# Polysketch attention and a SwiGLU block on one core: chunk 1's weight splits on VectorE ahead of the numerators' copy, and two moves around the first later unit

## The chip, the cores and the metric

The kernel runs on one core of a Trainium2 chip. The metric is the device time of one execution in microseconds, the median of several runs. The times of the profile come from one profiled execution of the same program.

## The reference

Four batches of four heads, 1088 positions and head size 32 go through an attention with sketched features; the result (4352 tokens of 128 values) goes through a gated feed-forward block with 1536 hidden columns.

```python
def phi(x):
    a = einsum('rd,bhsd->bhsr', S1, x); b = einsum('rd,bhsd->bhsr', S2, x)   # r = 8
    return einsum('bhsi,bhsj->bhsij', a, b).reshape(..., 64)
kv  = einsum('bhsf,bhsd->bhfd', phi(k), v);  z = phi(k).sum(axis=2)
num = einsum('bhsf,bhfd->bhsd', phi(q), kv)
den = einsum('bhsf,bhf->bhs', phi(q), z)[..., None] + 1e-06
x   = (num / den).transpose(0, 2, 1, 3).reshape(4352, 128)
g   = x @ w_gate
out = (g / (1 + exp(-g)) * (x @ w_val)) @ w_out
```

## The kernel before

The feed-forward block works on the transposed tokens `xT`, 128 values by 4352 tokens. The tokens are cut into blocks: blocks 0, 1 and 2 hold the first batch (384, 320 and 384 tokens), and block 3 (`HEAD`) and the ones behind it hold 480 tokens each, the last 384. The hidden columns are cut into 12 pieces of 128. A *unit* is one block with one piece: gate and value products, the sigmoid-weighted gate, and their product in a hidden slot (`hbuf` or `late`). A *down product* multiplies one hidden slot by its 128 rows of `w_out` and sums the 12 of a block in one PSUM bank; then `store` turns the block on VectorE (L1110) and SyncE's queue writes it out.

From the middle of block 2 on, a unit is made of three faster products in the place of one full fp32 product. The weights are split for it in chunks of three pieces (`cut_weights`, L839 to L855): ScalarE makes the high part `w1` (L843); an engine that is passed in makes the rest `low` = w - `w1` (L846); ScalarE scales it to `wb` (L848); and the difference part `wd` follows on VectorE as an L851 (from `low` and `w1`) or on GpSimd as an L855 (from `w1` and `wb`). The tokens are split in the same manner by `cut_tokens` (L865 on ScalarE; L868 and L873). Each generator stops after each step, and `at(...)` takes the next step of those it names, so the tables `steps_at` in the main part set by hand where each step is issued. The engines each run their instructions in the order in which they are issued.

`start_unit` (L974) takes a pair of PSUM banks, runs the two difference products (L980), and ScalarE rescales both banks in place (L983). `finish_unit` (L985) adds four products (L992, L993), ScalarE applies the sigmoid form (L995), VectorE multiplies into the hidden slot (L1000), and the pair is given back. Three pairs of banks go round, and the attention takes pairs from the same three.

The attention of batches 1 to 3 is the generator `attentions` (L615), of which `parts_of(1)` takes one step and `group()` a step with work for TensorE. Around the change the order is this. `numerators(1)` (L766) lets TensorE multiply the turned query features by the values' sums (L776, after the last L758) and copies the result into `xT`, half on ScalarE and half on VectorE (both L793). Then `cut_tokens` splits block 3's tokens, whose `xd` the first difference product of block 3 reads. `features` (L703) makes the key features of batch 2 on VectorE in four pieces (L377), in three steps: piece 1; pieces 2 and 3; piece 4. GpSimd sums these features in five additions (L547), and the keys and queries of later batches are turned on VectorE (L327, L578).

The loop `while todo` (L1350) works off the last down products of blocks 0 to 2. When seven are left, one step of the attention and the token split are taken; at four and three left, one step each; at two left the first unit of block 3 is started. Then the loop over `y` (L1375) runs the later units: it starts unit y + 1, finishes unit y, takes up to two down products, one step of the attention, and due token splits; a group comes before y = 4. `finish_unit` runs what `add_to(behind, y, f)` has left for y just after its L1000.

Of the kernel before, what the change touches and what calls it, by code (L numbers as in the profile page):

```python
# [19 lines left out]
def kernel(  # L20
# [28 lines left out]
    nc = tc.nc  # L49
# [62 lines left out]
    def bank(tag=None):  # L112

        if tag is not None:
            i = place[tag]
        else:
            i = place[free_banks[turn[0] % len(free_banks)]]
            turn[0] += 1
        touch(i)
        return PS[:, i, :]  # L120
# [29 lines left out]
    wg = const.tile([P, NCH, P], FP32, name="wg")  # L150
    wv = const.tile([P, NCH, P], FP32, name="wv")
# [645 lines left out]
    HEAD = len(steps)  # L797
    hidden = {}
    acc = {}
    todo = []  # L800
# [16 lines left out]
    def whole(ap):  # L817
        return ap.bitcast(FP32)
# [10 lines left out]
    def home(w, c):  # L829


        if w is wg:
            return [big("phq", k) if k < 4 else big("raw", k - 4) for k in range(3 * c, 3 * c + 3)]
        return [
            stage.tile([P, 3, P], F32R, tag=tag, name=name, bufs=6)[:]
            for tag, name in (("exp", "w1"), ("man", "wb"), (("exp", "man")[c % 2], "wd"))
        ]

    def cut_weights(w, c, low, engine):  # L839

        w1, wb, wd = w_parts[id(w), c] = home(w, c)
        src = w[:, 3 * c : 3 * c + 3, :]
        nc.scalar.activation(out=w1, in_=src, func=AF.Copy, scale=CUT)  # L843
        yield
        low = low[0]
        engine.tensor_tensor(out=low, in0=src, in1=whole(w1), op=ALU.subtract)  # L846
        yield
        nc.scalar.activation(out=wb, in_=low, func=AF.Copy, scale=BETA)  # L848
        yield
        if engine is nc.vector:  # L850
            nc.vector.scalar_tensor_tensor(  # L851
                out=wd, in0=low, scalar=-BETA, in1=whole(w1), op0=ALU.mult, op1=ALU.add
            )
        else:
            engine.tensor_tensor(out=wd, in0=whole(w1), in1=whole(wb), op=ALU.subtract)  # L855

    def cut_tokens(i, engine=nc.gpsimd, soon=False):

        t0, n = blocks[i]
        x = xT[:, t0 : t0 + n]  # L860
        x1, x0, xd = x_parts[i] = [
            apool.tile([P, WB], F32R, tag=tag, name=name, bufs=2)
            for tag, name in (("qb", "x1"), ("dT", "x0"), ("rd", "xd"))
        ]
        nc.scalar.activation(x1[:, 0:n], x, AF.Copy, scale=CUT)  # L865

        def low():
            engine.tensor_tensor(  # L868
                out=x0[:, 0:n], in0=x, in1=whole(x1[:, 0:n]), op=ALU.subtract
            )  # L870

        def difference():
            nc.vector.scalar_tensor_tensor(  # L873
                out=xd[:, 0:n], in0=whole(x1[:, 0:n]), scalar=WHOLE, in1=x,
                op0=ALU.mult, op1=ALU.subtract,
            )


        first, second = (difference, low) if soon else (low, difference)
        first()  # L880
        yield
        second()
# [10 lines left out]
    before, behind = {}, {}  # L893

    def add_to(where, y, f):
        where.setdefault(y, []).append(f)
# [77 lines left out]
    def start_unit(i, j):  # L974

        n = blocks[i][1]
        xd = x_parts[i][2][:, 0:n]
        ps = sums_of[i, j] = pair((i, j))[:, :, 0:n]
        for k, w in enumerate((wg, wv)):
            nc.tensor.matmul(  # L980
                ps[:, k], w_parts[id(w), j // 3][2][:, j % 3, :], xd, start=True, stop=True
            )
        nc.scalar.activation(ps, ps, AF.Copy, scale=-1.0 / WHOLE)  # L983
# [61 lines left out]
    def down(y=None):  # L1045

        i, j = todo.pop(0)
        n = SPLIT if i == LAST else blocks[i][1]
        first = i not in acc
        if first:  # L1050
            acc[i] = bank("g2" if i == 1 or i in line[2::2] else "acc")
        made[i] = made.get(i, 0) + 1
        mine = [c for c in range(NCH) if (i, c) in DOWN]
        if mine and j == mine[0]:
            acc[i, "p"] = bank("acc" if i in line[2::2] else "g2")
        sides = dict(start=first, stop=(made[i] == NCH))
        if j in mine:
            w1, wb, wd = [down_parts[x][:, FINE.index(j), :] for x in ("w1", "wb", "wd")]
            h1, h0, hd = h_parts.pop((i, j))
            nc.tensor.matmul(acc[i][:, 0:n], wd, hd, **sides)  # L1060
            p = acc[i, "p"][:, 0:n]
            nc.tensor.matmul(p, w1, h1, start=(j == mine[0]), stop=False)  # L1062
            nc.tensor.matmul(p, wb, h0, start=False, stop=(j == mine[-1]))  # L1063
            if j == mine[-1]:
                copy_out(y, i, n)
        else:
            w = down_parts["scaled"][:, PLAIN.index(j), :] if mine else wo[:, j, :]
            nc.tensor.matmul(acc[i][:, 0:n], w, hidden[i, j][:, 0:n], **sides)  # L1068
        if i != LAST:
            hidden.pop((i, j))  # L1070
            slots.append(slot_of[i, j])
        if made[i] == NCH:
            if mine:
                put_together(y, i, n)
            else:
                store(i, n)

    def copy_out(y, i, n):

        x = fpool.tile([P, WB], FP32, tag="sg", name="sum2", bufs=5)[:, 0:n]  # L1080
        p = acc[i, "p"][:, 0:n]
        acc[i, "p"] = x
        add_to(behind, y + 1, lambda: nc.scalar.activation(x, p, AF.Copy, scale=WHOLE))

    def put_together(y, i, n):

        d, x = acc.pop(i)[:, 0:n], acc.pop((i, "p"))
        acc[i] = x
        add_to(before, y + 1, lambda: nc.vector.scalar_tensor_tensor(
            out=x, in0=d, scalar=-1.0, in1=x, op0=ALU.mult, op1=ALU.add  # L1090
        ))
        add_to(before, y + 2, lambda: store(i, n))
# [13 lines left out]
    def store(i, n):  # L1106
        t0 = blocks[i][0]

        o = fpool.tile([P, WB // 32, 32], FP32, tag="o", name="o", bufs=2)
        nc.vector.transpose(  # L1110
            out=o[:, 0 : n // 32, :], in_=acc.pop(i)[:, 0:n].rearrange("p (x t) -> p x t", t=32)
        )
        t1 = t0 + n
        while t0 < t1:
            b, x0 = divmod(t0 // 32, NX)
            m = min(t1 - t0, S * (b + 1) - t0) // 32
            k = (t0 - blocks[i][0]) // 32
            for a in range(4):
                queue = nc.scalar if i == LAST and a % 2 else nc.sync
                queue.dma_start(  # L1120
                    out=rows[b, a, :, x0 : x0 + m, :],
                    in_=o[32 * a : 32 * a + 32, k : k + m, :],
                )
            t0 += 32 * m
# [55 lines left out]
    n = steps[0][1]  # L1180
# [50 lines left out]
    def parts_of(n):  # L1231

        for _ in range(n):
            if ahead[0] not in ("pe", "end"):
                ahead[0] = next(att, "end")
# [37 lines left out]
    def free(c):  # L1273
        return [room[:, c, :].rearrange("p (c f) -> p c f", f=P)]
# [13 lines left out]

    cuts = {"x": cut_tokens(2, nc.vector, soon=True)}
    for c in (2, 3, 0, 1):  # L1290
        cuts["g%d" % c] = cut_weights(wg, c, free(8 + c % 2), nc.vector if c > 1 else nc.gpsimd)
        cuts["v%d" % c] = cut_weights(wv, c, free(6 + c % 2), nc.gpsimd)

    def at(*names):
        for name in names:
            next(cuts[name], None)

    def next_down():
        if order:
            todo.remove(order[0])  # L1300
            todo.insert(0, order.pop(0))
        down()

    steps_at = {20: ("v2",), 21: ("v3", "v2", "v3"), 22: ("g2",), 23: ("g3",)}
    for z, (i, j) in enumerate(seq):
# [16 lines left out]
    steps_at = {  # L1322
        0: ("g2", "v2", "v3"), 1: ("g2",), 2: ("g2", "g3"), 3: ("g3", "v2"), 4: ("g3", "v3"), 5: ("g2",),
        7: ("x",), 8: ("x", "g3", "v0"), 9: ("g0",), 10: ("v0",), 11: ("g0",),
    }
    ND = 13
    for n in range(ND):
# [7 lines left out]


    steps_at = {
        9: ("v0",), 10: ("g0", "v0"), 11: ("g0",),
    }
    todo.sort(key=lambda x: (order + [x]).index(x))  # L1340
    for j in range(6, NCH):
# [4 lines left out]
        parts_of(1)  # L1346
        at(*steps_at.get(j, ()))
    x_steps = iter(())
    steps_at = {7: ("v1", "g1", "v1", "g1"), 6: ("v1", "g1"), 1: ("v1", "g1")}
    while todo:  # L1350
        if len(todo) == 2:
            start_unit(HEAD, 0)
        next_down()
        at(*steps_at.get(len(todo), ()))
        next(x_steps, None)
        if len(todo) == 7:
            parts_of(1)
            x_steps = cut_tokens(HEAD, nc.vector, soon=True)
            next(x_steps)
        if len(todo) in (3, 4):  # L1360
            parts_of(1)

    flat = hbuf[:].rearrange("p s w -> p (s w)")
# [73 lines left out]
```

## Time and profile before

| What | Value |
|---|---|
| median of three runs | 278.69 us (278.63 to 278.96) |
| the profiled execution, whole | 278.54 us |
| its span, first to last instruction | 276.8 us |
| TensorE busy, 85 to 90 us | 4.68 of 5 |
| TensorE busy, 90 to 95 us | 5.00 of 5 |
| TensorE busy, 95 to 100 us | 4.31 of 5 |
| VectorE busy, 90 to 95 and 95 to 100 us | 4.77 and 4.80 of 5 |
| GpSimd busy, 85 to 90, 90 to 95, 95 to 100 us | 1.87, 3.33, 4.05 of 5 |
| TensorE clock granted | 1.0 of full speed |

Times in the trace count from the span's start. A row of a timeline gives start, duration, engine, the line of the kernel, the operation, what it writes and reads, and in brackets how long the engine stood idle before it and who ended that. Matmuls are pipelined, so their durations overlap; the distance between two starts is the pace.

### The profile page before, as it was taken

How to read it: one execution, taken by the hardware profiler on the slowest of the kernel's cores; microseconds unless marked ns; L12 is line 12 of the kernel's file. 1: busy time of each engine (PE TensorE's matmuls, PEld its weight loads, DVE VectorE, ACT ScalarE, POOL GpSimd, SP SyncE). 2: the span in 40 equal slices, each digit the busy share in tenths (PEclk: the TensorE clock that was granted, in tenths of full speed). 3: DMA queues.
4: the chain of work that ended last, by engine and by line, in shares of the span. 5: the costliest groups of instructions: out<-in, count | busy, mean ns of one | idle time of the engine just before them, and what ended most of it. 6: DMA issues, size and time to landing. Idle time of an engine off the chain costs nothing.

```text
span 276.8 us, 5724 instructions
## 1 busy us (share of the span) xinstructions
PE 269.6 (97%) x2181; PEld 200.0 (72%) x2181; DVE 208.5 (75%) x353; ACT 189.9 (69%) x337; POOL 104.6 (38%) x114
## 2 busy tenths in 40 slices
PE   7899999999999999999999999999999999999995
PEld 7645566667885676777577777867887888788994
DVE  3997988799896983887545766967978995987431
ACT  3468566372684766667479898768879878886860
POOL 3314322159925650160034353435425553542000
PEclk9999999999999999999999999999999999999999
DMA  6573195222240124000200020000100200010011
GB/s 193 168 229 92 38 282 176 83 81 83 42 97 12 30 56 124 2 0 0 38 12 5 2 37 0 0 2 11 26 2 0 36 0 1 17 21 1 9 29 28
DMA packets 26139, 14.30 MB, mean 52 GB/s; under 512 B 19840, under 2 KB 24192, under 8 KB 26112
## 3 DMA queue, kind: packets, MB, share of 16 engines
q1 hardware_dynamic: 25456, 13.84, 19.6%
q8 instruction: 17, 0.28, 0.4%
q10 hardware_dynamic: 656, 0.10, 0.2%
q14 instruction: 10, 0.08, 0.1%
HBM read 11.41 MB, written 2.23 MB: 49 GB/s over the span
## 4 chain that ended last, share of the span: by engine, by line
PE 91%; DVE 4%; DMA 1%; issue 1%; ACT 1%; SPq 0%; DVEq 0%
PE PS L1068 21%; PE PS L980 14%; PE PS L992 14%; PE PS L993 13%; PE PS L1016 12%; PE PS L1063 2%; PE PS L1060 2%; PE PS L1062 2%; PE PS L354 2%; PE PS L776 2%; PE PS L342 2%; PE PS L388 2%; DMA kld<-in_k_dram 1%; PE PS L1096 1%; PE PS L497 1%
## 5 line engine op out<-in xcount | busy, mean ns | idle before, releaser
L983 ACT ACTIVATE PS<-PS 128x960 f32<-128x960 f32 (+1 forms) x90 | 83.3, 925 | 33.7 <-PE PS L980 32.9
L1000 DVE SCALAR_TENSOR_TENSOR hbuf<-PS,sg 128x480 f32<-128x480 f32 (+1 forms) x87 | 55.3, 635 | 42.3 <-ACT sg L995 39.8
L995 ACT ACTIVATE sg<-PS 128x480 f32<-128x480 f32 (+1 forms) x90 | 49.6, 551 | 2.1 <-PE PS L993 1.2
L1068 PE MATMUL PS<-hbuf,wo 128*128 128x480 f32 (+3 forms) x118 | 45.9, 488 | 0.0
L980 PE MATMUL PS<-xd,graw 128*128 128x480 f32 (+1 forms) x69 | 38.2, 554 | 0.0
L980 PE MATMUL PS<-xd,wd 128*128 128x480 f32 (+1 forms) x90 | 33.6, 373 | 0.7 <-DVE hbuf L1000 0.7
L993 PE MATMUL PS<-x,wb 128*128 128x480 f32 (+1 forms) x90 | 33.5, 372 | 0.0
L992 PE MATMUL PS<-x,w 128*128 128x480 f32 (+1 forms) x90 | 33.4, 371 | 0.0
L1068 PEld LDWEIGHTS PS<-hbuf,wo 128*128 128x128 f32 x118 | 22.0, 189 | 5.6 <-issue 0.4
L993 PE MATMUL PS<-x,graw 128*128 128x480 f32 (+1 forms) x69 | 25.5, 370 | 0.0
L980 PEld LDWEIGHTS PS<-xd,wd 128*128 128x128 f32 x90 | 17.0, 189 | 11.4 <-issue 6.0
L1016 PE MATMUL PS<-xT,wg 128*128 128x384 f32 (+1 forms) x60 | 23.5, 474 | 0.1
L1016 PE MATMUL PS<-xT,wv 128*128 128x384 f32 (+1 forms) x60 | 23.1, 467 | 0.3 <-DVE wv L286 0.3
L868 POOL TENSOR_TENSOR x<-xT,x 128x480 fp32r<-128x480 f32 (+1 forms) x6 | 7.2, 1195 | 37.4 <-ACT x L865 37.3
L1020 ACT ACTIVATE sg<-PS 128x384 f32<-128x384 f32 (+1 forms) x24 | 11.2, 468 | 13.2 <-PE PS L1016 12.4
L980 PEld LDWEIGHTS PS<-xd,graw 128*128 128x128 f32 x69 | 13.0, 188 | 7.7 <-ACT PS L983 4.1
L992 PEld LDWEIGHTS PS<-x,w 128*128 128x128 f32 x90 | 16.9, 187 | 2.2
L993 PEld LDWEIGHTS PS<-x,wb 128*128 128x128 f32 x90 | 16.9, 188 | 2.1
L992 PE MATMUL PS<-x,graw 128*128 128x480 f32 (+1 forms) x48 | 18.4, 383 | 0.0
L1068 PE MATMUL PS<-hbuf,scaled 128*128 128x480 f32 x36 | 17.4, 564 | 0.0
L960 POOL TENSOR_TENSOR hlate<-hbuf,hlate 128x480 fp32r<-128x480 f32 x10 | 12.9, 1291 | 9.8 <-ACT hlate L959 7.7
L1016 PEld LDWEIGHTS PS<-xT,wv 128*128 128x128 f32 x60 | 11.2, 190 | 7.4 <-DVE hbuf L1031 0.8
(196 smaller groups left out, 545.0 us busy)
## 6 DMA issues: line engine op xcount, KB each, us to landing
kld<-in_k_dram SPq DMA_DIRECT2D x4, 544.0 KB, 4.1
vld<-in_v_dram SPq DMA_DIRECT2D x12, 144.0 KB, 4.0
qld<-in_q_dram SPq DMA_DIRECT2D x3, 544.0 KB, 3.6
raw<-in_moe_w_out_dram SPq DMA_DIRECT2D x4, 384.0 KB, 4.2
raw<-in_moe_w_gate_dram SPq DMA_DIRECT2D x3, 384.0 KB, 3.6
raw<-in_moe_w_val_dram SPq DMA_DIRECT2D x3, 384.0 KB, 3.7
out_dram<-o SPq DMA_DIRECT2D x16, 60.0 KB, 1.9
vld<-in_v_dram SPq DMA_DIRECT2D x4, 112.0 KB, 4.1
```

What stands on the lines that cost most here:

```text
L342: nc.tensor.matmul(ps[32 * a : 32 * a + 32, 96 * (c - c0) : 96 * (c - c0) + 96], qT[:, 4 * c + a, :], s123[:, a : a + H, :, :].rearrange(" ...
L868: engine.tensor_tensor(out=x0[:, 0:n], in0=x, in1=whole(x1[:, 0:n]), op=ALU.subtract)
L960: add_to(before, y + 2, lambda: nc.gpsimd.tensor_tensor(out=h0, in0=h, in1=whole(h1), op=ALU.subtract))
L980: nc.tensor.matmul(ps[:, k], w_parts[id(w), j // 3][2][:, j % 3, :], xd, start=True, stop=True)
L983: nc.scalar.activation(ps, ps, AF.Copy, scale=-1.0 / WHOLE)
L992: nc.tensor.matmul(ps[:, k], w1, x1, start=False, stop=False, skip_group_check=True)
L993: nc.tensor.matmul(ps[:, k], wb, x0, start=False, stop=True, skip_group_check=True)
L995: nc.scalar.activation(sg, ps[:, 0], AF.Silu, scale=WHOLE)
L1000: nc.vector.scalar_tensor_tensor(out=hj[:, 0:n], in0=ps[:, 1], scalar=WHOLE, in1=sg, op0=ALU.mult, op1=ALU.mult)
L1016: nc.tensor.matmul(o[:, 0:n], w[:, j, :], xT[:, t0 : t0 + n], start=True, stop=True)
L1020: nc.scalar.activation(sg[:, 0:n], g[:, 0:n], AF.Silu)
L1068: nc.tensor.matmul(acc[i][:, 0:n], w, hidden[i, j][:, 0:n], **sides)
```

## The change

There are three edits. Chunk 1's parts of both weights are made on VectorE instead of GpSimd, and its steps are issued earlier: the high parts and the rests right after piece 11 of block 2, the scaling and the difference parts when nine and eight down products are left, all ahead of `numerators(1)` and its copies; before, they were issued while the last down products ran, from seven left to one left. The turn and the writing of block 2's output is no longer issued with its last down product, but left for the place behind the product of unit 1 of the later units. And one more step of the attention is taken in the loop `while todo`, so that all four feature pieces come ahead of the first later unit's product, and the steps behind them come one unit earlier, up to the group before y = 4.

```diff
         if made[i] == NCH:
             if mine:
                 put_together(y, i, n)
+            elif i == HEAD - 1:
+
+                add_to(behind, 1, lambda: store(i, n))
             else:
                 store(i, n)
...
-        cuts["g%d" % c] = cut_weights(wg, c, free(8 + c % 2), nc.vector if c > 1 else nc.gpsimd)
-        cuts["v%d" % c] = cut_weights(wv, c, free(6 + c % 2), nc.gpsimd)
+        cuts["g%d" % c] = cut_weights(wg, c, free(8 + c % 2), nc.vector if c else nc.gpsimd)
+        cuts["v%d" % c] = cut_weights(wv, c, free(6 + c % 2), nc.vector if c == 1 else nc.gpsimd)
...
     steps_at = {
-        9: ("v0",), 10: ("g0", "v0"), 11: ("g0",),
+        9: ("v0",), 10: ("g0", "v0"), 11: ("g0", "v1", "g1", "v1", "g1"),
     }
...
-    steps_at = {7: ("v1", "g1", "v1", "g1"), 6: ("v1", "g1"), 1: ("v1", "g1")}
+    steps_at = {9: ("v1", "g1"), 8: ("v1", "g1")}
     while todo:
...
-        if len(todo) in (3, 4):
+        if len(todo) in (2, 3, 4):
             parts_of(1)
```

In the order of instructions, TensorE and SyncE keep theirs. ScalarE has the same instructions, with chunk 1's two L848 ahead of its copy L793 and not behind the token split L865. GpSimd loses four instructions and keeps the order of the rest. VectorE's order around the place is:

| before | after |
|---|---|
| L758 | L758 |
| | L846, L846, L851, L851 (chunk 1) |
| L793, L873, L868 | L793, L873, L868 |
| L377 x3, L1110 (block 2), L1000, L377 | L377 x4, L1000 |
| L1000, L327 | L327, L1000, L1110 (block 2) |
| L1000, L327, L1000, L578, L578 | L327, L1000, L578, L1000, L578 |

## The prediction

> **What bounds the kernel now.** I read the page first, then the list of what TensorE waited for, then the timelines of TensorE, VectorE, GpSimd and ScalarE between 76 and 104 us, where every moved instruction lies. I call the later units (the loop over y, block 3 onwards) U0, U1, U2, U3, U4.
>
> The page's line of the engines, and two of TensorE's waits over the whole span (us in total, times, longest):
>
> ```profile
> PE 269.6 (97%) x2181; PEld 200.0 (72%) x2181; DVE 208.5 (75%) x353; ACT 189.9 (69%) x337; POOL 104.6 (38%) x114
> ```
> ```profile
> PE PS L980 <- DVE hbuf L1000: 0.7, 1, 0.7
> ...
> PE PS L776 <- DVE phT L758: 0.3, 1, 0.3
> ```
>
> TensorE is the bound: work taken off other engines counts only where TensorE waits for it. Its largest wait on another engine is for the product of a later unit (L1000), which gives the bank pair of U1 back for U4. TensorE's timeline there (start, duration):
>
> ```profile
> 96.20 0.38 PE L980 MATMUL PS<-xd,graw 128*128 128x480 f32 x1
> 97.27 0.49 PE L980 MATMUL PS<-xd,wd 128*128 128x480 f32 x1 [0.69 <-DVE hbuf L1000]
> 97.59 0.38 PE L992 MATMUL PS<-x,gphq 128*128 128x480 f32 x1
> ...
> 98.55 1.21 PE L388 MATMUL PS<-phk,vld 128*32 128x64 f32 x72
> ```
>
> Matmuls of this form follow each other at 0.22 us (98.02 to 98.24, L992 to L993), so the second L980 could have started at 96.42: the wait costs 97.27 - 96.42 = 0.85 us, and the restart (97.27 to 97.59 instead of 0.22) 0.1 us more. Why L1000 came late, on VectorE:
>
> ```profile
> 84.56 0.96 DVE L758 STREAM_TRANSPOSE phT<-phq 128x768 f32<-128x768 f32 x1
> 87.24 0.69 DVE L793 COPY xT<-PS 128x512 f32<-128x512 f32 x1 [1.72 <-PE PS L776]
> 88.66 0.66 DVE L873 SCALAR_TENSOR_TENSOR xd<-x,xT 128x480 fp32r<-128x480 f32 x1 [0.73 <-ACT x L865]
> 89.23 1.45 DVE L868 TENSOR_TENSOR x<-xT,x 128x480 fp32r<-128x480 f32 x1
> 90.61 2.96 DVE L377 TENSOR_TENSOR phk<-kab 128x768 f32<-128x768 f32 x3
> 93.49 0.57 DVE L1110 STREAM_TRANSPOSE o<-PS 128x384 f32<-128x384 f32 x1
> 94.29 0.66 DVE L1000 SCALAR_TENSOR_TENSOR hbuf<-PS,sg 128x480 f32<-128x480 f32 x1 [0.23 <-ACT sg L995]
> 94.87 1.78 DVE L377 TENSOR_TENSOR phk<-kab 128x512 f32<-128x512 f32 x1
> 96.57 0.65 DVE L1000 SCALAR_TENSOR_TENSOR hbuf<-PS,sg 128x480 f32<-128x480 f32 x1
> ```
>
> ScalarE had U1's sigmoid ready much earlier, and GpSimd was busy in the same time:
>
> ```profile
> 95.03 0.57 ACT L995 ACTIVATE sg<-PS 128x480 f32<-128x480 f32 x1
> ```
> ```profile
> 89.12 1.05 POOL L855 TENSOR_TENSOR wd<-w,wb 128x384 fp32r<-128x384 f32 x1 [3.13 <-ACT wb L848]
> 90.14 1.41 POOL L855 TENSOR_TENSOR graw<-gphq,graw 128x384 fp32r<-128x384 f32 x1
> 93.14 1.59 POOL L547 TENSOR_TENSOR zs<-phk 128x512 f32<-128x512 f32 x1 [1.59 <-DVE phk L377]
> 94.81 1.29 POOL L547 TENSOR_TENSOR zs<-zs,phk 128x512 f32<-128x512 f32 x1
> ```
>
> The reader is to see: U1's sigmoid ended at 95.60, its product began only at 96.57, and in between VectorE was in the fourth feature piece, which took 1.78 us where the third, alone, took 0.68 (92.89 in a narrower window). GpSimd's sum ran from 94.81 to 96.10, and the piece's last 0.68 began about as it ended.
>
> [...] L377 1.78 against 0.68, L868 1.45 beside L855, while L1000 (one input in PSUM) kept 0.66 beside the sum that ran until 94.73. [...]
>
> **The change, part by part.**
>
> *Splits.* Four GpSimd instructions go (L846 twice, 83.39 to 85.99, the first held back by L377; L855 twice, 89.12 to 91.55), and four VectorE ones come between L758, over at 85.52, and L793. Their inputs (L843 on ScalarE) are ready at 83.73. GpSimd is idle there now, its last work before being the L855 that ends at 83.35[...]. Price: [...] two L851 at 0.587 (the one row of before without GpSimd beside it; two rows are 587 and 995). Starts follow 0.06 earlier than ends here (82.52 + 1.65 = 84.17 against 84.09), so the sum is 2 x 0.50 + 2 x 0.53 = 2.05 us: from 85.46 to 87.51. VectorE idled 1.72 us there, so the copy L793 begins at 87.5 instead of 87.24: 0.27 late. ScalarE's two L848 move into its 3.45 us of idle before its own L793 and are over at about 87.1; it isn't late.
>
> The chain behind the copy: L865 at 88.3, L873 from 88.93 to 89.6. TensorE reads that at 90.11, behind down products without a wait, so 0.27 of its 0.77 slack is used: cost nothing. If that cover were gone, each 0.1 us would cost 0.1. Then L868 runs without GpSimd's L855: [...] from 89.5 to 90.15, half a microsecond earlier than before. POOL's queue loses four instructions; nothing queued behind them (the sums) was waiting for them. Chunk 1's parts are ready at 87.5; TensorE first reads one at 94.81.
>
> *Features in front of U0's product.* Four pieces: 0.95 + 3 x 0.68, less 3 x 0.06. Piece 1 from 90.1 (before, it waited for L855 until about 91.5), piece 2 until 91.65, piece 3 until 92.25. The first sum [...] at 92.2 to 93.45 (1.27); piece 4, issued at 92.2, waits for it and ends at about 94.0. If the sum comes in ahead of piece 3, piece 4 ends near 94.15. Either is before U0's sigmoid ends (93.69 + 0.57 = 94.26), so L1000 of U0 stays at 94.29. Behind it now stands the key transpose (0.83[...]): over at 95.71. L1000 of U1 then starts at 95.66 and ends at 96.31; TensorE wants the bank at 96.42. The wait of 0.85 is gone.
>
> *The output's turn.* 0.57 us leaves the place ahead of U0's product, where 0.23 of idle followed it, and comes behind U1's: about 96.25 to 96.8. The second key transpose behind it ends at 97.5 (before 99.13) and is read at 98.9 or so. The accumulator bank it frees is written again at 103.87. Its four DMAs stay where they are in SP's queue, ahead of the query load issued at 101.35; a few microseconds of issue from 96.8 fit. Cost nothing.
>
> *One more attention step.* The first key transpose and the query transposes come one unit earlier; both query transposes stood in a row ahead of `fold` (99.89 to 101.32), which waits for TensorE's L713 (101.21) anyway. No gain, no loss.
>
> *What is late next.* U4's rescaling on ScalarE (L983) needs the sigmoid of U2 (to 96.96) and TensorE (96.9): level, and only needed after the attention group. U3's first L992 needs L983 that ended at 96.48; TensorE comes there at 96.64. The group's L713 needs GpSimd's sums: with piece 4 at 94.0 they end near 98.4, TensorE asks at 100. So the gain stays in TensorE's stream, whose order is the same to the end.
>
> Sum: -0.85 for the wait, and of the restart's 0.1 I take 0.03, since a weight load that waits even briefly (95.00) showed 0.09 of lost pace too. -0.88 on the profiled 278.54 (span 276.8, 1.74 around it) gives 277.66; that execution lies 0.15 under the median 278.69, for which I say 277.8. Bounds: -1.0 if the restart goes fully and U0's pace gains, -0.5 if U1's product slips by 0.35 more than worked out.
>
> **Rivals.**
>
> [...] (no gain). Piece 4 then waits for the second sum as well, to 94.7, and ends at 95.35; U0's product ends at 95.95 and U3's second L980 starts at 96.0 instead of 95.03, 0.97 late; U1's product, after the transpose, ends at 97.3, in time for what TensorE then wants at 97.39. Against 97.27 that is 0.1 lost: 278.8. [...] Against it, VectorE and GpSimd in an earlier stretch:
>
> ```profile
> 64.02 1.20 DVE L846 TENSOR_TENSOR room<-wg,graw 128x384 f32<-128x384 f32 x1
> ```
> ```profile
> 63.53 2.81 POOL L547 TENSOR_TENSOR zs<-zs,phk 128x512 f32<-128x512 f32 x2
> ```
>
> The waiting difference finished at 65.22, between the two sums, which end at 66.34: the waiter got its turn.
>
> *The splits are slow on VectorE* (slower). Every L846 that before shows there took 1.09 to 1.20, and L851 0.79 on average: 2 x 1.14 + 2 x 0.79 - 0.24 = 3.6 us. The copy starts at 89.1, xd ends at 91.2, TensorE waits 1.1 us at U0's first product and some 0.1 at U0's bank, and the 0.88 is still won: 278.69 + 0.3 = 279.0. It decides from about 3.4 us for the four (2.5 is where the wait starts, plus the 0.88). Against it: those rows all overlap GpSimd's sums, and here GpSimd is empty from 83.35 to 91.75.
>
> *A partial gain*: U0's product slips behind piece 4 by a few tenths, 278.2.
>
> **How the numbers follow.** Forecast 0.77, [...] partial 0.05, slow splits 0.08, something unseen that is slower 0.03. The forecast's own range is 277.5 to 278.1; the range reaches over the partial and the no-gain case: 277.4 to 278.8. A measurement tells 0.2% (0.56 us) from no change. Faster: 0.77 and a little of the partial, 0.78; same 0.11; slower 0.11.
>
> **What would show it.** Right: the list of TensorE's waits has no L980 behind L1000; L793 on VectorE at about 87.5; L868 near 0.65; four pieces ending before 94.3; U1's product at about 95.7; the group's L388 at about 97.7. Wrong: L846 on VectorE above 0.8; a wait of L980 for xd near 90; U0's product after 94.6; or L388 early and the gain given back before 104 us, at L713 or L342.

## The result and the profile after

The median is 277.69 us (277.58 to 277.91, six runs) against 278.69 us of the kernel before beside it: a ratio of 0.9963, 95% interval 0.9950 to 0.9976, or 1.0 us less. The profiled execution took 277.69 us, with a span of 276.0 us. Measured again later (change_again), the changed kernel had 277.85 against 278.68 us (0.9967, 0.9955 to 0.9980).

TensorE's waits of the changed kernel (us in total, times, longest), from the longest down:

```profile
PE PS L241 <- PEq L1424: 0.9, 1, 0.9
...
PE PS L354 <- DVE kT L327: 0.3, 1, 0.3
PE PS L776 <- DVE phT L758: 0.3, 1, 0.3
```

No L980 waits behind L1000 any more; the wait of L776 has stayed. (The wait of L354 lies at 6 us, ahead of everything that was moved; it was 0.6 before and goes up to 1.1 in the kernels below, so it says nothing about the change.) TensorE's timeline at the place (start, duration):

```profile
90.21 0.67 PE L980 MATMUL PS<-xd,gphq 128*128 128x480 f32 x1
...
96.28 0.39 PE L980 MATMUL PS<-xd,graw 128*128 128x480 f32 x1
96.51 0.42 PE L980 MATMUL PS<-xd,wd 128*128 128x480 f32 x1
96.77 0.38 PE L992 MATMUL PS<-x,gphq 128*128 128x480 f32 x1
...
97.73 1.21 PE L388 MATMUL PS<-phk,vld 128*32 128x64 f32 x72
```

The two L980 from 96.28 on are 0.23 us apart instead of 1.07. The attention group's L388 starts at 97.73 instead of 98.55; this execution was 0.11 us behind the other at the last L758 (84.67 against 84.56), so the stretch between is 0.93 us shorter. VectorE in the changed kernel:

```profile
84.67 0.96 DVE L758 STREAM_TRANSPOSE phT<-phq 128x768 f32<-128x768 f32 x1
85.56 0.51 DVE L846 TENSOR_TENSOR room<-wv,w 128x384 f32<-128x384 f32 x1
86.00 0.54 DVE L846 TENSOR_TENSOR room<-wg,gphq 128x384 f32<-128x384 f32 x1
86.46 0.54 DVE L851 SCALAR_TENSOR_TENSOR wd<-room,w 128x384 fp32r<-128x384 f32 x1
86.93 0.54 DVE L851 SCALAR_TENSOR_TENSOR graw<-room,gphq 128x384 fp32r<-128x384 f32 x1
87.40 0.68 DVE L793 COPY xT<-PS 128x512 f32<-128x512 f32 x1
88.81 0.66 DVE L873 SCALAR_TENSOR_TENSOR xd<-x,xT 128x480 fp32r<-128x480 f32 x1 [0.73 <-ACT x L865]
89.38 0.65 DVE L868 TENSOR_TENSOR x<-xT,x 128x480 fp32r<-128x480 f32 x1
89.95 3.85 DVE L377 TENSOR_TENSOR phk<-kab 128x768 f32<-128x768 f32 x4
94.39 0.66 DVE L1000 SCALAR_TENSOR_TENSOR hbuf<-PS,sg 128x480 f32<-128x480 f32 x1 [0.59 <-ACT sg L995]
...
95.73 0.66 DVE L1000 SCALAR_TENSOR_TENSOR hbuf<-PS,sg 128x480 f32<-128x480 f32 x1
```

Chunk 1's splits take 0.51 to 0.54 us each on VectorE; the two L846 that VectorE ran before, for other chunks and beside GpSimd's sums, took 1.09 and 1.20. L868 takes 0.65 instead of 1.45. All four feature pieces are over at 93.80, ahead of U0's sigmoid, and U1's product starts at 95.73 instead of 96.57. GpSimd in the changed kernel has nothing from 83.46 to 91.67:

```profile
91.67 1.57 POOL L547 TENSOR_TENSOR zs<-phk 128x512 f32<-128x512 f32 x1 [8.21 <-DVE phk L377]
93.32 3.00 POOL L547 TENSOR_TENSOR zs<-zs,phk 128x512 f32<-128x512 f32 x2
```

### The profile page after: what moved, and what is told of

The parts are those of the page before. It is cut to its first block, busy times and chain, and to the rows that moved or that the text cites. A ratio compares the mean times of both kernels' runs of the same rounds, so it can differ in the third digit from the quotient of the medians.

```text
span 276.0 us, 5718 instructions
## 1 busy us (share of the span) xinstructions
PE 269.7 (98%) x2181; PEld 200.1 (73%) x2181; DVE 208.4 (76%) x357; ACT 189.9 (69%) x337; POOL 99.9 (36%) x110
## 4 chain that ended last, share of the span: by engine, by line
PE 91%; DVE 4%; DMA 2%; issue 1%; ACT 1%; SPq 0%
PE PS L1068 21%; PE PS L980 14%; PE PS L992 14%; PE PS L993 13%; PE PS L1016 12%; PE PS L1063 2%; PE PS L1060 2%; PE PS L1062 2%; PE PS L354 2%; PE PS L776 2%; PE PS L342 2%; PE PS L388 2%; DMA kld<-in_k_dram 2%; PE PS L1099 1%; PE PS L497 1%
## 5 line engine op out<-in xcount | busy, mean ns | idle before, releaser
L1000 DVE SCALAR_TENSOR_TENSOR hbuf<-PS,sg 128x480 f32<-128x480 f32 (+1 forms) x87 | 55.2, 635 | 42.5 <-ACT sg L995 40.0
L980 PE MATMUL PS<-xd,graw 128*128 128x480 f32 (+1 forms) x69 | 38.2, 553 | 0.0
L980 PE MATMUL PS<-xd,wd 128*128 128x480 f32 (+1 forms) x90 | 33.5, 372 | 0.0
L992 PE MATMUL PS<-x,w 128*128 128x480 f32 (+1 forms) x90 | 33.4, 371 | 0.0
L980 PEld LDWEIGHTS PS<-xd,wd 128*128 128x128 f32 x90 | 17.0, 189 | 10.4 <-issue 6.0
L868 POOL TENSOR_TENSOR x<-xT,x 128x480 fp32r<-128x480 f32 (+1 forms) x6 | 7.1, 1191 | 38.3 <-ACT x L865 38.3
L980 PEld LDWEIGHTS PS<-xd,graw 128*128 128x128 f32 x69 | 13.0, 188 | 7.7 <-ACT PS L983 4.1
L992 PEld LDWEIGHTS PS<-x,w 128*128 128x128 f32 x90 | 16.9, 187 | 2.2
L992 PE MATMUL PS<-x,graw 128*128 128x480 f32 (+1 forms) x48 | 18.4, 383 | 0.0
L1016 PEld LDWEIGHTS PS<-xT,wg 128*128 128x128 f32 x60 | 10.9, 190 | 7.7 <-issue 1.1
```

The lines of the kernel that those rows point to most:

```text
L868: engine.tensor_tensor(out=x0[:, 0:n], in0=x, in1=whole(x1[:, 0:n]), op=ALU.subtract)
L980: nc.tensor.matmul(ps[:, k], w_parts[id(w), j // 3][2][:, j % 3, :], xd, start=True, stop=True)
L992: nc.tensor.matmul(ps[:, k], w1, x1, start=False, stop=False, skip_group_check=True)
L1000: nc.vector.scalar_tensor_tensor(out=hj[:, 0:n], in0=ps[:, 1], scalar=WHOLE, in1=sg, op0=ALU.mult, op1=ALU.mult)
L1016: nc.tensor.matmul(o[:, 0:n], w[:, j, :], xT[:, t0 : t0 + n], start=True, stop=True)
```

## The experiments

The change has three parts that could each have earned the time. Theory A: GpSimd's late splits held back VectorE's token split and first feature piece (before, L868 took 1.45 us beside L855), and everything behind them on VectorE came late; taking them out of that stretch is the whole gain. Theory B: the order earns it, with the features in front of U0's product and the output behind U1's. The times:

| kernel | median, us | before beside it, us | ratio (95%) |
|---|---|---|---|
| splits_alone | 277.78 | 278.61 | 0.9966 (0.9955 to 0.9977) |
| moves_alone | 278.67 | 278.61 | 1.0003 (0.9992 to 1.0014) |
| splits_gpsimd_early | 277.66 | 278.61 | 0.9966 (0.9955 to 0.9976) |
| no_output_move | 277.74 | 278.61 | 0.9964 (0.9951 to 0.9977) |
| splits_twice | 279.42 | 278.66 | 1.0025 (1.0019 to 1.0032) |
| chunk0_later | 277.54 | 278.66 | 0.9952 (0.9936 to 0.9968) |
| change_again | 277.85 | 278.68 | 0.9967 (0.9955 to 0.9980) |
| chunk0_later_again | 277.29 | 278.68 | 0.9952 (0.9940 to 0.9965) |
| chunk0_splits_only | 277.30 | 278.68 | 0.9953 (0.9940 to 0.9967) |

All edits below are against the changed kernel.

**The splits alone** (splits_alone):

```diff
-            elif i == HEAD - 1:
-
-                add_to(behind, 1, lambda: store(i, n))
...
-        if len(todo) in (2, 3, 4):
+        if len(todo) in (3, 4):
```

> Chunk 1's splits on VectorE ahead of the copy, as in the change; the third block's output is turned where it was, and the fourth feature piece stays behind U0's product. Theory A ([...] GpSimd's late splits held back VectorE's token split and first feature piece): with the splits gone GpSimd's first two sums are over at about 94.8, the fourth piece takes about 0.68 us from about 95.0, U1's product starts at about 95.7, TensorE has no wait of L980 behind L1000, and the median is 277.6 to 277.9, all of the gain. Theory B (the order pays: features in front of U0's product, output behind U1's): the wait stays at 0.4 us or more and the median is 278.3 to 278.8.

Measured: 277.78 us. VectorE around U0's and U1's products in this kernel:

```profile
92.54 0.58 DVE L1110 STREAM_TRANSPOSE o<-PS 128x384 f32<-128x384 f32 x1 [0.33 <-PE PS L1068]
94.50 0.66 DVE L1000 SCALAR_TENSOR_TENSOR hbuf<-PS,sg 128x480 f32<-128x480 f32 x1 [1.38 <-ACT sg L995]
95.07 0.68 DVE L377 TENSOR_TENSOR phk<-kab 128x512 f32<-128x512 f32 x1
95.85 0.66 DVE L1000 SCALAR_TENSOR_TENSOR hbuf<-PS,sg 128x480 f32<-128x480 f32 x1
```

GpSimd's first two sums:

```profile
91.78 1.58 POOL L547 TENSOR_TENSOR zs<-phk 128x512 f32<-128x512 f32 x1 [8.22 <-DVE phk L377]
93.44 1.29 POOL L547 TENSOR_TENSOR zs<-zs,phk 128x512 f32<-128x512 f32 x1
```

The fourth piece stands between the two products, where it stood before the change, and takes 0.68 us instead of 1.78: GpSimd's first two sums are over at 94.73, because they could start 1.4 us earlier. VectorE even has 1.38 us of idle ahead of U0's product. Chunk 1's splits alone, on the other engine and at the earlier place, earn the gain; which of these two it is, the next kernels tell.

**The moves alone** (moves_alone):

```diff
-        cuts["g%d" % c] = cut_weights(wg, c, free(8 + c % 2), nc.vector if c else nc.gpsimd)
-        cuts["v%d" % c] = cut_weights(wv, c, free(6 + c % 2), nc.vector if c == 1 else nc.gpsimd)
+        cuts["g%d" % c] = cut_weights(wg, c, free(8 + c % 2), nc.vector if c > 1 else nc.gpsimd)
+        cuts["v%d" % c] = cut_weights(wv, c, free(6 + c % 2), nc.gpsimd)
...
-        9: ("v0",), 10: ("g0", "v0"), 11: ("g0", "v1", "g1", "v1", "g1"),
+        9: ("v0",), 10: ("g0", "v0"), 11: ("g0",),
...
-    steps_at = {9: ("v1", "g1"), 8: ("v1", "g1")}
+    steps_at = {7: ("v1", "g1", "v1", "g1"), 6: ("v1", "g1"), 1: ("v1", "g1")}
```

> The features' and the output's move alone; chunk 1's splits stay on GpSimd and where they were before. Theory A: GpSimd's L855 still hold L868 and the first feature piece, the first sum [...] holds the fourth piece until about 94.7, U0's product starts at about 95.3 and not 94.3, TensorE waits about 1 us at U3's second L980 in place of U4's, and the median is 278.6 to 279.0, no gain. Theory B: the median is 277.6 to 278.0.

Measured: 278.67 us, no gain. VectorE, and then TensorE, in this kernel:

```profile
89.39 1.45 DVE L868 TENSOR_TENSOR x<-xT,x 128x480 fp32r<-128x480 f32 x1
90.76 4.66 DVE L377 TENSOR_TENSOR phk<-kab 128x768 f32<-128x768 f32 x4
95.34 0.65 DVE L1000 SCALAR_TENSOR_TENSOR hbuf<-PS,sg 128x480 f32<-128x480 f32 x1
```
```profile
94.96 0.38 PE L980 MATMUL PS<-xd,graw 128*128 128x480 f32 x1
96.04 0.48 PE L980 MATMUL PS<-xd,wd 128*128 128x480 f32 x1 [0.70 <-DVE hbuf L1000]
```

L868 is as slow as before the change, U0's product starts at 95.34 although its sigmoid ended at 94.41, and the same wait of 0.70 us, a gap of 1.08 between the two L980, now stands at U3 instead of U4. Without the splits out of the way, the moves only shift the wait by one unit.

**The splits early, but on GpSimd** (splits_gpsimd_early):

```diff
-        cuts["g%d" % c] = cut_weights(wg, c, free(8 + c % 2), nc.vector if c else nc.gpsimd)
-        cuts["v%d" % c] = cut_weights(wv, c, free(6 + c % 2), nc.vector if c == 1 else nc.gpsimd)
+        cuts["g%d" % c] = cut_weights(wg, c, free(8 + c % 2), nc.vector if c > 1 else nc.gpsimd)
+        cuts["v%d" % c] = cut_weights(wv, c, free(6 + c % 2), nc.gpsimd)
```

> All as in the change, but chunk 1's splits stay on GpSimd, issued at the new early places. Theory A in its narrow form (what counts is that GpSimd is out of the way before VectorE's token split at about 89 us, not which engine makes the splits): GpSimd makes them from 83.5 to about 88.1, while VectorE idles or copies from PSUM; L868 takes 0.65 us, the wait for U1's product is gone, the copy L793 starts about 0.15 us earlier than in the change, and the median is 277.6 to 277.9. The rival (the engine counts, GpSimd is too slow and stays in the way): L868 or the first feature piece takes over 1.2 us and the median is 278.2 to 278.8.

Measured: 277.66 us. GpSimd's splits in this kernel:

```profile
83.58 1.63 POOL L846 TENSOR_TENSOR room<-wv,w 128x384 f32<-128x384 f32 x1
85.17 1.00 POOL L846 TENSOR_TENSOR room<-wg,gphq 128x384 f32<-128x384 f32 x1
86.12 1.01 POOL L855 TENSOR_TENSOR wd<-w,wb 128x384 fp32r<-128x384 f32 x1
87.08 1.01 POOL L855 TENSOR_TENSOR graw<-gphq,graw 128x384 fp32r<-128x384 f32 x1
```

VectorE's token split behind them:

```profile
88.85 0.66 DVE L873 SCALAR_TENSOR_TENSOR xd<-x,xT 128x480 fp32r<-128x480 f32 x1 [0.73 <-ACT x L865]
89.42 0.65 DVE L868 TENSOR_TENSOR x<-xT,x 128x480 fp32r<-128x480 f32 x1
```

GpSimd takes about twice as long for each (1.00 and 1.01 us for the last three; the first, beside VectorE's L377, took 1.63) and is still through at 88.09, ahead of L873. The copy L793 came only 0.04 us earlier than in the change, counted from L758, where 0.15 was expected. So it is not the engine that counts, but when GpSimd's splits run: here ahead of L868 (0.65 us), in moves_alone its two L855 (89.27 to 91.69) ran beside L868 (1.45). This kernel and moves_alone differ only in when chunk 1's steps are issued: in the traces of the two, the one order that differs is ScalarE's, whose two L848 run ahead of its copy L793 instead of behind its token split L865. That is 277.66 against 278.67 us. ScalarE itself was not late in moves_alone: behind these L848 it stood idle for 1.59 us, waiting for TensorE. Both kernels have the two moves; the early splits on GpSimd without the moves, and the splits on VectorE at their old late place, were not run.

**Without the output's move** (no_output_move):

```diff
-            elif i == HEAD - 1:
-
-                add_to(behind, 1, lambda: store(i, n))
```

> The change without the output's move: the third block's output is turned with its last down product, ahead of U0's product. Theory A: the turn (0.57 us) fits into the 0.59 us for which VectorE idles ahead of U0's product in the changed kernel, U0's product starts at 94.3 to 94.5, and the median is that of the change, 277.6 to 277.9. The rival (the output's move earns part of the gain): U0's product or U1's comes 0.3 us or more later and the median is 278.0 to 278.4.

Measured: 277.74 us. VectorE, and then ScalarE's sigmoid of U0, in this kernel:

```profile
93.76 0.57 DVE L1110 STREAM_TRANSPOSE o<-PS 128x384 f32<-128x384 f32 x1
94.43 0.66 DVE L1000 SCALAR_TENSOR_TENSOR hbuf<-PS,sg 128x480 f32<-128x480 f32 x1
```
```profile
93.83 0.57 ACT L995 ACTIVATE sg<-PS 128x480 f32<-128x480 f32 x1
```

The turn is over at 94.33, the sigmoid at 94.40, and U0's product starts at 94.43: the move earns nothing that can be seen. It takes 0.57 us of work out of a place where VectorE is otherwise idle.

**The splits twice** (splits_twice): each split instruction of chunk 1 is issued twice.

```diff
-        engine.tensor_tensor(out=low, in0=src, in1=whole(w1), op=ALU.subtract)
+        for _ in range(2 if c == 1 else 1):
+            engine.tensor_tensor(out=low, in0=src, in1=whole(w1), op=ALU.subtract)
...
-            nc.vector.scalar_tensor_tensor(
-                out=wd, in0=low, scalar=-BETA, in1=whole(w1), op0=ALU.mult, op1=ALU.add
-            )
+            for _ in range(2 if c == 1 else 1):
+                nc.vector.scalar_tensor_tensor(
+                    out=wd, in0=low, scalar=-BETA, in1=whole(w1), op0=ALU.mult, op1=ALU.add
+                )
```

> The change with each of chunk 1's four split instructions on VectorE issued twice, so that they take about 4.0 us in place of 2.0. By the prediction's sum the copy L793 starts about 1.85 us later, the token difference xd ends at about 91.3, and TensorE, which reads it at 90.2, waits about 1.2 us at U0's first product (start of the wait at 2.5 us for the four); median 278.8 to 279.1, slightly slower than the kernel before. The rival (the copy has more slack than worked out, since down products or other work can fill TensorE): the median stays under 278.2. A second rival (each 0.1 us of the splits is paid from the first on): 279.5 or more.

Measured: 279.42 us, 0.76 slower than the kernel before; the expectation was missed by 0.3. The copy's start and TensorE's first difference product in this kernel (the edit moves its lines: L982 is L980, L875 is L873, L867 is L865):

```profile
89.64 0.68 DVE L793 COPY xT<-PS 128x512 f32<-128x512 f32 x1
91.05 0.66 DVE L875 SCALAR_TENSOR_TENSOR xd<-x,xT 128x480 fp32r<-128x480 f32 x1 [0.73 <-ACT x L867]
```
```profile
91.85 0.46 PE L982 MATMUL PS<-xd,gphq 128*128 128x480 f32 x1 [1.31 <-DVE xd L875]
```

From the first split (85.43) to the copy it is 4.21 us, against 1.84 in the change: 2.37 more, where I had expected 1.85. Each of the four pairs takes 1.02 to 1.07 us to the start of what follows it (starts at 85.43, 86.45, 87.51 and 88.58); in the change two splits in a row take 0.90 and 0.94.

The mechanism holds. In the change `xd` ends at 89.47 and TensorE starts on it at 90.21, without a wait; here it ends at 91.71 and TensorE, which waited, starts at 91.85, 0.14 later. So 0.74 - 0.14 = 0.60 us of the copy's delay is free and 1.77 is paid: from the first split to TensorE's product it is 6.42 us instead of 4.65. At L388, 1.66 of it is left (99.26 against 97.73, and this execution was 0.13 ahead of the other at the last L758), and the medians differ by 1.57 to 1.73. The first rival falls with that, since nothing fills TensorE behind the free part. The second would have all 2.37 us paid, a median of about 280.1. Its range began at 279.5 because it was worked out for a shorter delay; the median of 279.42 alone would hardly tell it apart, the trace does.

**Chunk 0's last gate split later** (chunk0_later, then chunk0_later_again beside the change):

```diff
-        9: ("v0",), 10: ("g0", "v0"), 11: ("g0", "v1", "g1", "v1", "g1"),
+        9: ("v0",), 10: ("v0",), 11: ("g0", "v1", "g1", "v1", "g1"),
...
-    steps_at = {9: ("v1", "g1"), 8: ("v1", "g1")}
+    steps_at = {9: ("g0", "v1", "g1"), 8: ("v1", "g1")}
```

> The change, and chunk 0's last gate split on ScalarE and GpSimd (scaling L848, difference L855) is issued one step later, behind the sigmoid of piece 11 of block 2. In the changed kernel that L855 (82.5 to 83.5) holds the third query feature piece L377 (1.65 us in place of 0.95), which delays the last L758, for which TensorE waits 0.3 us ahead of the numerators. Theory A [...]: L377 takes about 0.95 us, L758 ends about 0.7 us earlier, the wait of L776 behind L758 is gone, and the median is 0.25 to 0.35 us under the change: 277.3 to 277.5. The rival (the wait comes from something else, or ScalarE's later L848 and L843 make chunk 1's splits late): L776's wait stays or L793 comes no earlier, and the median is 277.6 to 278.0.

Measured: 277.54 us, between the two expectations. The trace is plainer than the time. VectorE, and then GpSimd, in this kernel:

```profile
82.47 0.94 DVE L377 TENSOR_TENSOR phq<-qab 128x768 f32<-128x768 f32 x1
83.33 0.55 DVE L1000 SCALAR_TENSOR_TENSOR late<-PS,sg 128x384 f32<-128x384 f32 x1
83.80 0.96 DVE L758 STREAM_TRANSPOSE phT<-phq 128x768 f32<-128x768 f32 x1
```
```profile
83.34 1.01 POOL L855 TENSOR_TENSOR gphq<-gphq 128x384 fp32r<-128x384 f32 x1 [1.61 <-ACT gphq L848]
```

In the change the same two instructions ran side by side:

```profile
82.63 1.65 DVE L377 TENSOR_TENSOR phq<-qab 128x768 f32<-128x768 f32 x1
```
```profile
82.46 1.00 POOL L855 TENSOR_TENSOR gphq<-gphq 128x384 fp32r<-128x384 f32 x1 [0.57 <-ACT gphq L848]
```

L377 takes 0.94 instead of 1.65, since GpSimd's L855 now comes as it ends. The last L758 starts at 83.80 instead of 84.67, the wait of L776 is gone from the list, and L388 starts at 97.20 instead of 97.73. L377 itself started 0.16 earlier here, so 0.37 us of that are the step's. The six times of this kernel (277.24 to 277.92) overlap those of the change, so the change, this kernel and one without the moves were measured once more, side by side.

> The changed kernel once more, so that it shares its runs of the kernel before with the two kernels beside it: 277.6 to 277.8, 0.85 to 1.0 us under the kernel before.

> The change with chunk 0's last gate split one step later, once more, beside the change itself. By the two traces TensorE reaches the attention group 0.37 us earlier than in the change (counted from the third query feature piece), so the median is to lie 0.25 to 0.4 us under that of the change beside it. If the step gives its gain back behind the stretch looked at, it lies within 0.1 us of it.

Measured: 277.85 and 277.29 us. The change is 0.83 us under the kernel before, just short of what was expected. The two are 0.56 apart, more than expected, and the five runs of each don't overlap (277.60 to 277.92, and 277.18 to 277.57). The size is better taken from the traces: the profiled executions took 277.92 and 277.25 us; of these 0.67 us, 0.29 lay between the two at the third query feature piece (82.85 against 82.56), ahead of the step, and 0.38 came by L388 (97.96 against 97.29), as in the first pair. The step's gain reaches the end. With or without the moves (see the next kernel) it is the best version found: 1.1 and 1.4 us under the kernel before in its two measurements.

**Both clearing steps without the moves** (chunk0_splits_only): the two edits of splits_alone on top of chunk0_later.

> [...] (chunk 1's splits early on VectorE, chunk 0's last gate split later), without the features' and the output's move. If the moves earn nothing, as the earlier runs say, it is within 0.15 us of the kernel with them; if they do earn something once the other waits are gone, it is 0.2 us or more slower.

Measured: 277.30 against 277.29 us. The moves earn nothing here either.

## Why the prediction was right

The forecast was 277.8 and the time is 277.69, inside the forecast's own range. By its steps:

- *The wait of 0.85 us goes, and some of the restart*: right. The stretch got 0.93 us shorter against the 0.88 summed. L980 to L992 is 0.26 us instead of 0.32, so 0.06 of the restart's 0.1 came back, where I took 0.03. The two L980 are 0.84 us closer; the last 0.03 of the 0.93 lie ahead of them.
- *The splits, 2.05 us with GpSimd idle*: right in that none of them was slow (0.51 to 0.54 us each), the term a little too large. They took 1.84 us from first start to the copy, chiefly because each L851 lasted 0.54, not 0.587, and the two L846 took 0.44 and 0.46 to the next start where the sum has 0.50. That 0.50 was my estimate; no row of before shows an L846 on VectorE without GpSimd beside it. L377's rows of before, 0.68 us for 512 columns and 0.94 for 768, lead to 0.55 for 384, or 0.49 from start to start (an estimate). So the copy came hardly later: 0.05 us, counted from L758, instead of 0.27.
- *`xd` has 0.77 us of slack*: right for the change, which used 0.05 of it. The term was a little too large: TensorE starts 0.14 us after `xd` ends even where it waits for it, so that in splits_twice 0.60 us were free.
- *L868 falls to 0.65, the four pieces end at about 94.0, ahead of U0's sigmoid*: 0.65 and 93.80 (the 0.65 was my estimate; L873, of the same 480 columns, took 0.66 in before). *U1's product at about 95.7*: 95.73. *L388 at about 97.7*: 97.73.
- *The output's turn and the earlier attention steps cost and earn nothing*: right for the turn by no_output_move; for both by splits_alone.
- *The features in front of U0's product*: the prediction worked out their harmlessness but did not ask whether they were needed. They are not: splits_alone has the same time with the fourth piece in its old place. In moves_alone they shift the wait from U4 to U3.
- *The rival in which piece 4 also waits for the second sum* (given 0.07) didn't come: piece 4 ended at 93.80, 0.56 after the first sum, and the second ran until 94.95. *The rival "slow splits"* has its place confirmed by splits_twice, and its threshold fits: 4.21 us there cost 1.66 against a gain of 0.93, so that gain and cost would be level near 4.21 - 0.73 = 3.5 us (an estimate; the forecast said 3.4). But nothing slows the splits in the change, since GpSimd is empty there.

The prediction didn't see that chunk 0's L855 on GpSimd at 82.5 us was behind the wait that it left standing ahead of L776 (in chunk0_later, with that L855 at 83.34, L377 took 0.94 us and the wait was gone). The L377 of 1.65 us stood in the timeline, beside that L855, and I used its row only for the time at which it ends.

## What to carry to other kernels

When an elementwise instruction of VectorE takes two or three times its usual time (here 1.45 us instead of 0.65, and 1.78 instead of 0.68), look at what GpSimd ran at that moment (here an L855, and the second sum). Here the repair was not a faster instruction, but another time for the other engine's work. Issuing a small producer (here two scalings on ScalarE) ahead of a copy instead of behind it can move a whole chain on a third engine out of the way (277.66 us against 278.67). And try the parts of such a change alone: here one of three carried all of it, and with the other two in place it earned as much without changing the engine.

## What the runs showed of the hardware

In the changed kernel VectorE's third and fourth feature pieces meet GpSimd's first sums, and pieces and sums end in turn. The first sum starts at 91.67, while piece 3 runs (from 91.42), and takes 1.57 us, to 93.24; a sum of the same size beside an L1000 and an L327 took 1.28 in the kernel before (96.79). Piece 4, which starts at 92.02 in a narrower window, takes 1.77 us instead of 0.68 and ends at 93.80, 0.56 after that sum, although the second sum starts at 93.32. The two following sums took 3.00 us together: 1.63 for the second, to 94.95, and 1.30 for the third, which no piece met. The figures of no_output_move and splits_gpsimd_early are the same (2.99 and 3.00). What in the chip makes them end in turn, no run here shows.

I had also not expected that two equal VectorE splits in a row, into the same tile, take 1.02 to 1.07 us to the start of the next in splits_twice, where two into different tiles take 0.90 and 0.94 in the change (384 elements). Whether it is the write to the same place or a wait that goes with it was not tried.
